# A three-part kernel on TensorE: a new order for the second plan, GpSimd's later start in it, and the last output tile in two halves

## The chip, the cores and the metric

The kernel runs on one core of one Trainium2 chip. The metric is the device time of one execution in microseconds, taken as the median of repeated runs. One further execution is recorded by the hardware profiler; all rows below come from that one. In the rows PE is TensorE's matmuls, PEld its weight loads, DVE is VectorE, ACT ScalarE, POOL GpSimd and SP SyncE.

## The reference

Three layers follow each other; the output of each is the input of the next (float32).

```python
# attention: 4 batches, 8 heads, 576 tokens, 64 wide; block-causal mask in blocks of 64
scores = scale * np.matmul(q, k.transpose(0, 1, 3, 2))
scores = np.where(block_i >= block_j, scores, -1e9)
attn = softmax(scores); x = attn @ v            # reshaped to 2304 tokens x 512
# mixture of experts: 8 experts, 512 -> 1024 -> 512, the two best per token
noisy_logits = x @ w_gate + np.log1p(np.exp(x @ w_noise)) * noise
out[mask] += top2_w[mask, k, None] * (np.maximum(x[mask] @ w1[e], 0.0) @ w2[e])
# dense layer: 512 -> 2048 -> 512
h = x @ w_in
out = (h * np.clip(h + 3.0, 0.0, 6.0) / 6.0) @ w_out
```

## The kernel before

Every large product is made of three matmuls of two rounded parts each: a weight or activation is split into a high part (a cast, `hi`) and a low part (the difference, `lo`), and high x high, high x low and low x high are added up in PSUM. In the names `wah` and `wal` are the two parts of a piece of a first weight matrix, `wbh` and `wbl` of a second one, `xh` and `xl` of a transposed input, `hh` and `hl` of a hidden tile. ScalarE casts the high part of a weight (L408), VectorE or GpSimd subtracts for the low one (L412); L428 and L433 do the same for the input, L480 and L484 for the hidden tile. TensorE's s1 step is L457 to L459 (12 matmuls into a tile `h`), its s2 step L1122 to L1124 (6 matmuls for two token tiles, into tiles `y`).

The program has three stretches. In the first, attention of 16 pairs of heads goes through a first plan: a list scheduler (class `Plan`) that holds for each operation the engines it may run on with a cost, the operations it depends on, and a priority from the table `PR`. It walks through a modelled time, gives each free engine the ready operation of the lowest priority number, and writes the instructions in that order; each engine then runs its own instructions in order, and semaphores keep the dependences. `plan.run` returns the modelled time at which each engine is free.

The second plan begins where the first ends and takes these times as its start (`busy`). It holds three things. The first is the routing of the last batch of tokens (`route`): from the logits `lg` (L870) over softplus, top 2 and one-hot rows to `ohb`, the position matmuls on TensorE (L571 to L575), the selection rows `sel` and `rid`, the matmuls that list each expert's tokens (L616), and from them `ids` (L630). The second is the first 256 columns of expert 0, whose tokens are known from the first three batches: 8 s1 steps, 8 s2 steps, and the splits of its weights. The third follows from the routing: GpSimd gathers the rows of tiles 2 to 4 of expert 0 (L1091), TensorE transposes them (L425, two PSUM tiles in turn); a count of tokens per expert (L1409) leads to `ranks` on VectorE (L1381 to L1392) and `slot_rows` (L1398 to L1403), which fix the order of the experts and the row lists of the others. `PR` gives the priorities of all of these; `wl` picks an entry of `WLS`, the engines on which a weight's low part may run.

```python
WLS = ({"DVE": 1.2}, {"DVE": 1.14, "POOL": 2.4}, {"POOL": 2.4, "DVE": 1.14}, {"POOL": 2.4})
```

After the second plan the order is written out by hand: the rest of expert 0 in 368 columns, experts 1 to 7, then the dense layer. The weights of expert 1 are asked for from ScalarE's queue (L373, L375), its rows by GpSimd's gathers, both with numbers that `ranks` and `slot_rows` made. At the very end `m_s2` scales the four last output tiles from PSUM by 1/6, in turn on VectorE (L1499) and ScalarE (L1497), and SyncE's queue sends each of 256 KB to DRAM (L1502).

Of the kernel before, what the change touches and what calls it, by code (L numbers as in the profile page):

```python
# [7 lines left out]
F32 = mybir.dt.float32  # L8
# [6 lines left out]
OP = mybir.AluOpType  # L15
# [15 lines left out]
YB = 5  # L31
# [12 lines left out]
QSE = ({"DVE": 0.45}, {"POOL": 1.77}, {"ACT": 0.55}, {"DVE": 0.45, "ACT": 0.55})  # L44
WLS = ({"DVE": 1.2}, {"DVE": 1.14, "POOL": 2.4}, {"POOL": 2.4, "DVE": 1.14}, {"POOL": 2.4})
VHS = ({"POOL": 2.3}, {"DVE": 0.42}, {"POOL": 2.3, "DVE": 0.42}, {"DVE": 0.42, "POOL": 2.3}, {"ACT": 0.65, "DVE": 0.42})
PR = {'last': -400, 'ranks': 30, 'rows': -20.0, 'hold': 0.5, 'na': 185.6, 'nb': 352.4, 'lsel': (0, 0, 0, 0, 0, 0, 0, 1, 0, 0), 'f1': (-81.8, 24.7, 6.3, 59.0, -0.2, -63.6, -25.8, 17.6), 'f2': (-4.4, -9.0, -4.1, -76.6, 2.1, -7.1, 6.5, -47.2), 'fa': (-4.3, -4.4, -2.8, 81.4), 'fb': (10.5, -52.7, -45.1, -19.0), 'fh': (-82.6, 22.1, -3.3, -0.4, 24.6, -39.7, -3.6, -72.4), 'fl': (-15.2, 94.0, 43.5, -100.3, 0.8, -76.5, -19.7, 1.6), 'v': -315.73, 'qk': -55.37, 'keep': 1, 'S': 9.04, 'max': -280.34, 'exp': -161.48, 'pt': -15.17, 'hi': 83.56, 'hid': True, 'av': 18.28, 'o': -48.5, 'od': True, 'inv': -240.77, 'fin': 204.7, 'x': -99.74, 'route': 17.68, 'rp': 1, 'route2': -140.2, 'xt': -550.8, 'eg': 594.74, 'ex': 458.19, 'ew': 2239.12, 'first': 0, 'sel': 2, 'vh': 3, 'wl': 1, 'wa': -657.9, 'wb': -101.5, 'h': -105.8, 's2': -43.7, 'vs': (-20.6, 9.99, -35.58), 'vpt': (-0.86, 4.61, -5.4, -4.07, 10.04, 9.83, 18.45, -3.3), 'vp': (57.91, -8.69), 'vf': (23.48, -31.17), 'qe': 1, 'vmax': (-14.96, -14.1, 4.28, -1.49, -1.85, 1.55, -8.85, 4.24, 17.81), 'vexp': (8.68, -1.7, 10.68, 1.91, -0.09, 4.69, -24.46, 2.21, 0.2)}
CLAMP = 122879.9921875


# [7 lines left out]
class Plan:  # L58
# [11 lines left out]
    def add(self, eng, fn, deps=(), prio=0.0, take=None, drop=None, lat=None, after=0.0, port=False, kind=None):  # L70

        if drop is not None:
            drop.left += 1
        self.ops.append((eng, fn, {d for d in deps if d is not None}, prio, take, drop, lat, port, kind))
        self.ready.append(after)
        return len(self.ops) - 1
# [110 lines left out]
def kernel(  # L187
# [14 lines left out]
    nc = tc.nc  # L202
    B, H, S, D = v.shape
    N, DM = out.shape
# [13 lines left out]
    QC = [(0, BLK)] + [(BLK + 128 * i, 128) for i in range((S - BLK) // 128)]  # L218
# [178 lines left out]
    GR = [[(c, 0) for c in (1, 2)], [(c, 0) for c in range(3, NC)] + [(0, b) for b in range(0, B, 2)]]  # L397
# [6 lines left out]
    def split_hi(which, u, new=None):  # L404
        nm = "ab"[which]
        shape = [128, KD, 256] if which == 0 else [128, 2, DM]
        w_s[which, u] = (new or work_tile)(shape, f"w{nm}h"), (new or work_tile)(shape, f"w{nm}l")
        nc.scalar.copy(w_s[which, u][0], raws[PS[u]][which])  # L408
# [44 lines left out]
    yps = {}  # L453
# [43 lines left out]
    def route(b, dep, add, bank, psum, prio0, after=0.0):  # L497
# [8 lines left out]
        def tl(nm, shape=None, dt=F32, bufs=1):  # L506
            T[nm] = g_p.tile(shape or V, dt, tag=nm, name=nm, bufs=bufs)
            return T[nm]

        def step(nm, eng, fn, *deps, **kw):  # L510
            prio[0] += 0.25
            port = nm not in ("ez", "lu", "e2", "top", "ti", "pos", "t", "pi", "idm", "id", "os", "cnt", "short")
            dp[nm] = add(eng, fn, [dp[d] for d in deps] if deps else dep, prio[0], after=after, port=port, **kw)
# [5 lines left out]
        def eng_of(e):  # L519
            return nc.gpsimd if e == "POOL" else nc.vector  # L520
# [82 lines left out]
        for i in range(2):  # L603
# [4 lines left out]
            for c in range(NC):  # L608
                step(f"sel{i}{c}", (SELS[PR["lsel"][i * NC + c]] if last else {"POOL": 0.61}), lambda e, i=i, c=c: eng_of(e).tensor_scalar(
                    tl(f"sel{i}{c}", [128, 128], BF16), laneb, T["pmf"][:, i, c:c + 1], None, op0=OP.is_equal), "pmf")  # L610
# [47 lines left out]
    with actx:  # L658
# [69 lines left out]
        pt, oT, ri, xt = {}, {}, {}, {}  # L728

        def q_scale(e, p, c=(0, S)):  # L730
            o, i = qs[p % 2][:, c[0]:c[1]], raw["q", p % 2][:, c[0]:c[1]]
            if e == "ACT":
                nc.scalar.mul(o, i, qscale)
            else:
                engine(e).tensor_scalar(o, i, qscale, None, op0=OP.mult)

        def scores(p, u):
            q_, k_ = qs[p % 2], raw["k", p % 2]
            for i in ORDER[u]:
                for t, o, a, b_ in SEG[i]:  # L740
                    for h in range(2):
                        r = slice(64 * h, 64 * h + 64)
                        g = h ^ flip(i)
                        nc.tensor.matmul(sb[t][64 * g:64 * g + 64, o:o + b_ - a], lhsT=q_[r, i * BLK:(i + 1) * BLK],
                                         rhs=k_[r, a:b_], start=True, stop=True)
# [3 lines left out]
        def rowmax(p, i, m):  # L749
            if m == 0:  # L750
                nms[p, i] = sm_p.tile([128, len(SEG[i])], F32, tag=f"nm{len(SEG[i])}", name="nm")
            t, o, a, b_ = SEG[i][m]
            nc.vector.tensor_reduce(nms[p, i][:, m:m + 1], sb[t][:, o:o + b_ - a], axis=AX.X, op=OP.max, negate=True)  # L753
# [134 lines left out]
        for p in range(NPAIR):  # L888
            b, j = pairs[p]
            last = p == NPAIR - 1  # L890
# [16 lines left out]
            for m, c in enumerate(FIRST if p == 0 else ((0, S),)):  # L907
                n = c[1] - c[0]
                k["qs", p] = add({"DVE": 0.07 + n / 1500.0} if p == 0 else QSE[PR.get("qe", 0)], lambda e, p=p, c=c: q_scale(e, p, c),
                                 [k.get(("L", "q", p))] + sold, -50 + m if p == 0 else u0 + PR["qk"], after=LAND[m] if p == 0 else 0.0, port=p > 0)  # L910
                ready.append([k["qs", p], k.get(("L", "k", p))])
# [5 lines left out]
            for u in range(NU):  # L917
                U = u0 + u + PR["vs"][u]
                g = Bank(SPOOL[u], 1)
                k["S", p, u] = add({"PE": SCOST[u]}, lambda e, p=p, u=u: scores(p, u),  # L920
                                   ready[0] + (ready[-1] if u else []) + ([k["E", p, i] for i in (0, 1, 3)] if u == 2 else [k.get(("E", p - 1, 7))] if u == 0 else []), U + PR["S"], take=g, kind="S",
                                   after=LAND[min(u, 1)] + 0.1 if p == 0 else 0.0)
                ms, js = {}, {}
                for i in UN[u]:
                    for m, (t, o, a_, b_) in enumerate(SEG[i]):
                        ms[i, m] = add({"DVE": 0.07 + (b_ - a_) / 960.0}, lambda e, p=p, i=i, m=m: rowmax(p, i, m), [k["S", p, u]],
                                       U + PR["max"] + PR["vmax"][i])
                    js[i] = ms[i, 0]
# [31 lines left out]
            hold = add({"PE": 0.0}, lambda e: None, [k["O", p, 0], k["O", p, 1], set_, seti], U, take=gs[0], kind="S")  # L960
# [32 lines left out]
        busy = plan.run({"POOL": 3.6, "DVE": 2.6, "PE": 1.7 + 0.43 * WARM0, "ACT": 2.7, "SP": 2.3})  # L993
# [10 lines left out]
    work = ctx.enter_context(tc.tile_pool(name="work", bufs=2, reuse_waits="tile"))  # L1004
# [340 lines left out]
    def wops(which, u, deps, prio):  # L1345
        if (which, u) in PRE:
            return None
        hi = add({"ACT": 0.95}, lambda e: split_hi(which, u), deps, prio)
        return add(WLS[PR["wl"]], lambda e: split_lo(which, u, e), [hi], prio, port=True)
# [65 lines left out]
        xops(t, k2["g", t], PR["xt"] + t)  # L1415
    wops(0, NPF, [k2["s1", NF - 4], k2["s1", NF - 3]], PR["na"])
    wops(1, NPF, [k2["s2", NF - 4], k2["s2", NF - 3]], PR["nb"])
    plan2.run(busy, PR['last'] + 20, PR['hold'])
    gctx.close()
    wraw2[0] = ctx.enter_context(tc.tile_pool(name="wraw2", bufs=4, side="right", reuse_waits="tile"))  # L1420
# [69 lines left out]
    def m_s2(i, gi, f):  # L1490
        nt = len(GR[gi])
        s2(range(nt), hT.pop(("m", gi, f)), w_s[1, U0 + i], f, f == 0, f == NFF - 1)
        if f == NFF - 1:
            for t in range(nt):
                o = work.tile([128, DM], F32, tag="yo", name="yo", bufs=YB)
                if t % 2:
                    nc.scalar.mul(o, yps[t], 1.0 / 6.0)  # L1497
                else:
                    nc.vector.tensor_scalar(o, yps[t], 1.0 / 6.0, None, op0=OP.mult)  # L1499
                c, b = GR[gi][t]  # L1500
                if c:
                    nc.sync.dma_start(out[b * S + QC[c][0]:b * S + QC[c][0] + 128, :], o)  # L1502
                else:
                    for r in range(2):
                        nc.sync.dma_start(out[(b + r) * S:(b + r) * S + 64, :], o[r * 64:(r + 1) * 64])

    pairs2 = [(gi, p) for gi in range(len(GR)) for p in range(NFF // 2)]
    for i in range(len(pairs2) + 1):
        for r in range(2):
            if i < len(pairs2):  # L1510
                gi, p = pairs2[i]
                f = 2 * p + r
                nt = len(GR[gi + 1]) if gi + 1 < len(GR) else 0
# [11 lines left out]
            if i < len(pairs2) and gi + 1 >= TURNED:  # L1525
                t = (f - 6) // 2
                if f % 2 == 1 and 0 <= t < nt:
                    turned_tile((gi + 1, t, "m"), t, nt * 128, ("m", gi + 1))
                t = (f - 5) // 2
                if f % 2 == 0 and 0 <= t < nt:  # L1530
                    turn_out((gi + 1, t, "m"))
                t = (f - 3) // 2
# [38 lines left out]
```

## Time and profile before

| | |
|---|---|
| three runs | 1014.65 to 1015.74 us, median 1014.91 |
| the profiled execution | 1013.64 us, of which its span (first to last instruction) 1011.8 |
| TensorE busy in the span | 997.2 us (99%), 6813 matmuls |
| VectorE, ScalarE, GpSimd busy | 712.0, 558.3 and 253.4 us |
| mean granted TensorE clock | 0.996 |

A busy TensorE says that a matmul is under way, not that it runs at its peak. Idle time of the other engines costs nothing as such. What counts is where TensorE itself is idle or runs at the lower clock, and which engine's work ended that wait.

### The profile page before, as it was taken

The page shows a single profiled execution, that of the slowest core. Times are in us where ns is not written, and L with a number is a line of the kernel's source. Part 1 is how long each engine was busy: PE and PEld are TensorE (multiplying, and loading weights), DVE is VectorE, ACT ScalarE, POOL GpSimd, SP SyncE. Part 2 cuts the span into 40 slices and gives each one's busy share as a digit, 9 for nine tenths or more (in the row PEclk, how much of TensorE's full clock was granted, in tenths as well). Part 3 has the DMA queues.
Part 4 walks back from the last instruction along what each step waited for, and adds up shares of the span by engine and source line. Part 5 has one row for each costly group of instructions (what it writes and reads, how often), then busy time and mean ns, then how long its engine had stood idle before and what let it go on. Part 6 is the DMA issues. An engine that isn't in the chain of part 4 may idle for free. (4 is left out here: it accounts for less than half of the span.)

```text
span 1011.8 us, 18246 instructions
## 1 busy us (share of the span) xinstructions
PE 997.2 (99%) x6813; PEld 831.7 (82%) x6813; DVE 712.0 (70%) x1396; ACT 558.3 (55%) x1063; POOL 253.4 (25%) x353
## 2 busy tenths in 40 slices
PE   8999998999999999999999999999999999999998
PEld 5667666889889999998888989888888888888886
DVE  6686886767898999887878667757546745754542
ACT  6878785344656565655555356655445445444442
POOL 3255645141020302020200026615204401500000
PEclk9999999999999999999999999999999999999999
DMA  6656542189999999788884263122112202201001
GB/s 155 162 162 158 153 107 56 28 290 326 290 320 285 316 250 303 209 267 196 239 227 150 69 216 104 25 70 48 46 42 63 63 1 74 49 3 42 1 1 42
DMA packets 162745, 141.85 MB, mean 140 GB/s; under 512 B 91541, under 2 KB 130549, under 8 KB 162653
## 3 DMA queue, kind: packets, MB, share of 16 engines
q1 hardware_dynamic: 146669, 102.73, 36.6%
q0 software_dynamic: 8640, 28.32, 9.2%
q10 hardware_dynamic: 7344, 9.60, 2.8%
q8 instruction: 54, 0.88, 0.4%
q14 instruction: 38, 0.31, 0.1%
HBM read 92.91 MB, written 36.70 MB: 128 GB/s over the span
## 5 line engine op out<-in xcount | busy, mean ns | idle before, releaser
L458 PE MATMUL h<-xl,wah 128*128 128x512 f32 (+8 forms) x832 | 272.4, 327 | 3.0 <-DVE xl L433 3.0
L457 PE MATMUL h<-xh,wah 128*128 128x512 f32 (+8 forms) x832 | 273.3, 328 | 1.0 <-DVE lg L870 1.0
L459 PE MATMUL h<-xh,wal 128*128 128x512 f32 (+8 forms) x832 | 272.4, 327 | 0.0
L1122 PE MATMUL y<-wbh,hh 128*128 128x512 f32 (+1 forms) x576 | 226.0, 392 | 0.1
L1123 PE MATMUL y<-wbl,hh 128*128 128x512 f32 (+1 forms) x576 | 225.8, 392 | 0.0
L1124 PE MATMUL y<-wbh,hl 128*128 128x512 f32 (+1 forms) x576 | 225.1, 391 | 0.0
L458 PEld LDWEIGHTS h<-xl,wah 128*128 128x128 f32 x832 | 157.3, 189 | 17.9 <-DVE xl L433 3.4
L457 PEld LDWEIGHTS h<-xh,wah 128*128 128x128 f32 x832 | 157.3, 189 | 16.3 <-ACT wah L408 1.1
L459 PEld LDWEIGHTS h<-xh,wal 128*128 128x128 f32 x832 | 157.4, 189 | 11.5
L480 ACT ACTIVATE hh<-h 128x288 fp32r<-128x288 f32 (+7 forms) x128 | 53.0, 416 | 138.9 <-PE h L459 133.1
L1124 PEld LDWEIGHTS y<-wbh,hl 128*128 128x128 f32 (+1 forms) x576 | 107.5, 187 | 24.6
L1122 PEld LDWEIGHTS y<-wbh,hh 128*128 128x128 f32 (+1 forms) x576 | 107.6, 187 | 21.5 <-issue 0.6
L1123 PEld LDWEIGHTS y<-wbl,hh 128*128 128x128 f32 (+1 forms) x576 | 107.6, 187 | 20.7
L1485 DVE SCALAR_TENSOR_TENSOR r<-r,h 128x512 f32<-128x512 f32 (+1 forms) x80 | 50.4, 630 | 98.5 <-ACT r L1484 98.3
L1484 ACT ACTIVATE r<-h,three 128x512 f32<-128x512 f32 (+1 forms) x80 | 51.6, 645 | 119.0 <-PE h L459 119.0
L412 DVE TENSOR_TENSOR wal<-wa,wah 128x1024 fp32r<-128x1024 f32 x79 | 105.1, 1330 | 12.5 <-ACT wah L408 11.4
L412 DVE TENSOR_TENSOR wbl<-wb,wbh 128x1024 fp32r<-128x1024 f32 x75 | 101.3, 1351 | 14.9 <-ACT wbh L408 11.5
L408 ACT CAST wbh<-wb 128x1024 fp32r<-128x1024 f32 x80 | 83.8, 1047 | 24.8 <-PE y L1124 12.2
L1487 ACT CAST hh<-r 128x512 fp32r<-128x512 f32 (+1 forms) x80 | 46.2, 577 | 84.9 <-DVE r L1485 81.4
L1488 DVE TENSOR_TENSOR hl<-r,hh 128x512 fp32r<-128x512 f32 (+1 forms) x80 | 56.1, 701 | 51.5 <-ACT hh L1487 51.0
L762 ACT ACTIVATE P<-sb,nm 128x288 f32<-128x288 f32 (+8 forms) x160 | 78.7, 524 | 18.7 <-DVE nm L753 18.7
L408 ACT CAST wah<-wa 128x1024 fp32r<-128x1024 f32 x80 | 83.7, 1046 | 2.7 <-DMA wb<-in_moe_w_dram 1.8
(245 smaller groups left out, 1285.2 us busy)
## 6 DMA issues: line engine op xcount, KB each, us to landing
wa<-in_moe_w_dram SPq DMA_DIRECT2D x23, 512.0 KB
wb<-in_moe_w_dram SPq DMA_DIRECT2D x23, 512.0 KB
y_tab<-yo SPq DMA_DIRECT2D x32, 256.0 KB
w<-in_moe_w_in_dram SPq DMA_DIRECT2D x16, 512.0 KB
y_tab<-zero SPq DMA_DIRECT2D x8, 1024.0 KB
w<-in_moe_w_out_dram SPq DMA_DIRECT2D x16, 512.0 KB
wa<-in_moe_w_dram ACTq DMA_DIRECT2D x9, 512.0 KB
wb<-in_moe_w_dram ACTq DMA_DIRECT2D x9, 512.0 KB
```

What stands on the lines that cost most here:

```text
L408: nc.scalar.copy(w_s[which, u][0], raws[PS[u]][which])
L412: (nc.gpsimd if e == "POOL" else nc.vector).tensor_tensor(lo, raws[PS[u]][which], hi.bitcast(F32), op=OP.subtract)
L457: nc.tensor.matmul(ps, lhsT=wh, rhs=xh, start=first, stop=False)
L458: nc.tensor.matmul(ps, lhsT=wh, rhs=xl, start=False, stop=False)
L459: nc.tensor.matmul(ps, lhsT=wl, rhs=xh, start=False, stop=last)
L480: nc.scalar.activation(h[0][:, c0:c1], ps[:, :c1 - c0], AF.Relu)
L762: nc.scalar.activation(P[i][p % PB2][:, a:b_], sb[t][:, o:o + b_ - a], AF.Exp, bias=nms[p, i], scale=1.0, accum_out=rs[p % 3][:, COL[i] + ...
L1122: nc.tensor.matmul(yps[t][:n], lhsT=hh[:, sl], rhs=wh[:, f % 2], start=first, stop=False)
L1123: nc.tensor.matmul(yps[t][:n], lhsT=hh[:, sl], rhs=wl[:, f % 2], start=False, stop=False)
L1124: nc.tensor.matmul(yps[t][:n], lhsT=hl[:, sl], rhs=wh[:, f % 2], start=False, stop=last)
L1484: nc.scalar.activation(r[:, :n], ps[:, :n], AF.Relu, bias=three, scale=1.0)
L1488: nc.vector.tensor_tensor(hl[:, :n], r[:, :n], hh[:, :n].bitcast(F32), op=OP.subtract)
```

## The change

It has three parts. A line ahead of `plan2.run` sets GpSimd's start in the second plan to no sooner than the modelled end of VectorE's work in the first. The numbers of `PR` that belong to the second plan are replaced; among them `wl` goes from 1 to 0, which leaves the low parts of weights to VectorE alone, and `lsel` gives another one of the ten `sel` rows to GpSimd. In `m_s2` the last output tile is scaled in two halves of 256 columns, one by ScalarE and one by VectorE, and sent by two queues.

```diff
-PR = {'last': -400, 'ranks': 30, 'rows': -20.0, 'hold': 0.5,
...
-      'xt': -550.8, 'wl': 1, 'wa': -657.9, 'wb': -101.5, 'h': -105.8, 's2': -43.7,
+PR = {'last': -90, 'ranks': 30, 'rows': -100.0, 'hold': 0.7,
...
+      'xt': -1013.6, 'wl': 0, 'wa': -1003.9, 'wb': 69.6, 'h': -1.0, 's2': -203.8,
...
     wops(1, NPF, [k2["s2", NF - 4], k2["s2", NF - 3]], PR["nb"])
+    busy["POOL"] = max(busy["POOL"], busy["DVE"])
     plan2.run(busy, PR['last'] + 20, PR['hold'])
...
                 o = work.tile([128, DM], F32, tag="yo", name="yo", bufs=YB)
+                c, b = GR[gi][t]
+                if gi == len(GR) - 1 and t == nt - 1:
+                    r0 = b * S + QC[c][0]
+                    nc.scalar.mul(o[:, 0:DM // 2], yps[t][:, 0:DM // 2], 1.0 / 6.0)
+                    nc.scalar.dma_start(out[r0:r0 + 128, 0:DM // 2], o[:, 0:DM // 2])
+                    o2 = work.tile([128, DM], F32, tag="yo", name="yo", bufs=YB)[:, 0:DM // 2]
+                    nc.vector.tensor_scalar(o2, yps[t][:, DM // 2:], 1.0 / 6.0, None, op0=OP.mult)
+                    nc.sync.dma_start(out[r0:r0 + 128, DM // 2:], o2)
+                    continue
                 if t % 2:
                     nc.scalar.mul(o, yps[t], 1.0 / 6.0)
                 else:
                     nc.vector.tensor_scalar(o, yps[t], 1.0 / 6.0, None, op0=OP.mult)
-                c, b = GR[gi][t]
```

What the planner makes of the new numbers shows in the order of the instructions. The first place is VectorE where the second plan begins, as a piece of the difference (- before, + after): `xl_3019` belongs to expert 0's first columns, `zc` and `zx` are the first steps of the last batch's routing.

```order
 L859 TENSOR_TENSOR x<-tb_163,rn_205 128x5x64
 L433 TENSOR_TENSOR xl_3019<-tb_161,xh_3018 128x4x128
-L484 SCALAR_TENSOR_TENSOR hl<-h,hh 128x256
+L412 TENSOR_TENSOR wal<-wa,wah 128x1024
 L528 TENSOR_SCALAR zc<-lg_146 128x40
 L530 TENSOR_SCALAR zx<-lg_146 128x40
-L412 TENSOR_TENSOR wbl<-wb,wbh 128x1024
+L484 SCALAR_TENSOR_TENSOR hl<-h,hh 128x256
 L412 TENSOR_TENSOR wal<-wa,wah 128x1024
```

The routing's first steps now stand ahead of the first `hl`, which waits for TensorE; a weight's low part stands ahead of them. On GpSimd the two L412 rows of the second plan are gone, and nothing else of its order changes but which `sel` it makes. In this stretch TensorE gets four s1 and two s2 steps ahead of the fifth s1 and the position matmuls (L571), where it had two s1, one s2 and three s1.

The second place is TensorE at the end of the second plan; `xps` are the transposes of expert 0's gathered tiles, the first L457 with 128x368 begins its next columns. Before:

```order
L1124 MATMUL y_3142<-wbh,hl 128x512
L425 MATMUL xps<-ident,xn 128x128 x8
L1122 MATMUL y_3138<-wbh,hh 128x512
L1123 MATMUL y_3138<-wbl,hh 128x512
L1124 MATMUL y_3138<-wbh,hl 128x512
L1122 MATMUL y_3142<-wbh,hh 128x512
L1123 MATMUL y_3142<-wbl,hh 128x512
L1124 MATMUL y_3142<-wbh,hl 128x512
L457 MATMUL h<-xh,wah 128x368
```

And after the change:

```order
L1122 MATMUL y_3198<-wbh,hh 128x512
L1123 MATMUL y_3198<-wbl,hh 128x512
L1124 MATMUL y_3198<-wbh,hl 128x512
L425 MATMUL xps<-ident,xn 128x128 x8
L1409 LDWEIGHTS ones
L1409 MATMUL rps<-ohsum_131,ones 128x8
L457 MATMUL h<-xh,wah 128x368
```

The last s2 step has moved from behind the last transposes to ahead of them, and the count for the ranks (L1409) from ahead of the eighth s1 step to behind the transposes.

The third place is VectorE there, as a piece of the difference: the end of the rank block, the low parts of the gathered tiles (`xl`), and the first hidden tile of the 368 columns.

```order
 L1390 TENSOR_TENSOR me<-member,eio 128x64
 L1392 TENSOR_REDUCE order<-me 128x8
-L484 SCALAR_TENSOR_TENSOR hl<-h,hh 128x256
 L1398 SCALAR_TENSOR_TENSOR idf<-idacc 128x40
 L1400 TENSOR_TENSOR idt<-member,idf 128x320
 L1403 TENSOR_REDUCE sids<-idt 128x40
-L412 TENSOR_TENSOR wal<-wa,wah 128x1024
-L433 TENSOR_TENSOR xl<-xps,xh 128x4x128 x3
-L1135 COPY yo<-y_3138 128x512
 L412 TENSOR_TENSOR wal<-wa,wah 128x1024
 L484 SCALAR_TENSOR_TENSOR hl<-h,hh 128x368
```

Before, the three `xl` stood behind the rank block and one low part; now they stand ahead of it, and the block, with one low part, stands between the last `xl` and the first `hl` of the next stage.

## Rows read from the trace of the kernel before

**Rows 1.** Busy time by stage: stretch, PE, PEld, DVE, ACT, POOL, PEclk, DMA share, GB/s

```profile
170.00:210.00 40.00, 33.33 (x231) 29.76 (x221) 29.36 (x97) 15.14 (x26) 13.10 (x10) 0.91 0.19 50
210.00:250.00 40.00, 40.00 (x230) 35.77 (x230) 26.65 (x55) 19.23 (x29) 6.52 (x8) 1.00 1.00 339
250.00:1000.00 750.00, 749.79 (x3902) 645.03 (x3902) 529.51 (x832) 388.59 (x552) 149.72 (x125) 1.00 0.47 135
```

**Rows 2.** TensorE's waits: line, what ended them, us in total, times, longest

```profile
PE h L458 <- DVE xl L433: 3.0, 1, 3.0
PE rps L571 <- DVE ohb L523: 2.5, 1, 2.5
```

**Rows 3.** TensorE alone around its two waits: busy, PEclk, DMA share, GB/s

```profile
174.60:178.00 3.40, 3.13 (x14) 0.50 0.38 87
...
184.80:188.20 3.40, 0.88 (x11) 1.00 0.01 2
188.20:191.60 3.40, 3.40 (x14) 0.51 0.00 0
```

**Rows 4.** Timeline of GpSimd, 171 to 200 us: start, length, instruction, idle before

```profile
171.31 2.41 POOL L412 TENSOR_TENSOR wal<-wa,wah 128x1024 fp32r<-128x1024 f32 x1 [2.90 <-ACT wah L408]
...
196.68 1.63 POOL L1091 DMA_INDIRECT xn<-x_tok,ids  x1 [7.04 <-DVE ids L630]
...
199.88 0.95 POOL L1091 DMA_INDIRECT xn<-x_tok,ids  x1 [0.30 <-issue]
```

**Rows 5.** Timeline of VectorE, 171 to 187 us

```profile
171.27 2.55 DVE L870 TENSOR_TENSOR lg<-lg,x 128x80 f32<-128x80 f32 x2
...
174.14 0.68 DVE L433 TENSOR_TENSOR xl<-tb,xh 128x512 fp32r<-128x512 f32 x1
178.10 0.42 DVE L484 SCALAR_TENSOR_TENSOR hl<-h,hh 128x256 fp32r<-128x256 f32 x1 [3.29 <-ACT hh L480]
178.44 0.18 DVE L528 TENSOR_SCALAR zc<-lg 128x40 f32<-128x40 f32 x1
...
187.09 0.20 DVE L523 TENSOR_TENSOR ohb<-ohs 128x40 bf16<-128x40 f32 x1
```

**Rows 6.** Instructions of the tile lg on VectorE: shortest, median, longest in ns

```profile
L870 DVE TENSOR_TENSOR lg<-lg,x x2: 232/1256/2280, 171.3 to 171.5; 128x80 f32<-128x80 f32 x2
```

**Rows 7.** Timeline of VectorE, 195 to 201 us

```profile
195.47 0.24 DVE L627 TENSOR_TENSOR idacc<-idacc,rps 128x80 f32<-128x80 f32 x1 [1.35 <-PE rps L616]
...
197.76 0.16 DVE L1381 COPY counts<-rps 128x8 f32<-128x8 f32 x1
...
201.17 1.22 DVE L412 TENSOR_TENSOR wal<-wa,wah 128x1024 fp32r<-128x1024 f32 x1
```

**Rows 8.** Timeline of TensorE, 180 to 210 us

```profile
180.50 0.28 PE L457 MATMUL h<-xh,wah 128*128 128x256 f32 x1
...
184.59 0.28 PE L459 MATMUL h<-xh,wal 128*128 128x256 f32 x1
...
198.29 0.40 PE L1122 MATMUL y<-wbh,hh 128*128 128x512 f32 x1
...
201.05 0.60 PE L425 MATMUL xps<-ident,xn 128*128 128x128 f32 x4
...
202.88 1.38 PE L425 MATMUL xps<-ident,xn 128*128 128x128 f32 x8
...
205.66 0.44 PE L458 MATMUL h<-xl,wah 128*128 128x368 f32 x1
...
209.58 0.39 PE L1122 MATMUL y<-wbh,hh 128*128 128x512 f32 x1
```

**Rows 9.** Tail: last scaling on ScalarE (timeline), and busy time by stretch

```profile
1007.90 0.60 ACT L1497 ACTIVATE yo<-y 128x512 f32<-128x512 f32 x1 [0.76 <-PE y L1124]
...
1007.50:1010.00 2.50, 0.37 (x2) 0.00 (x0) 0.42 (x1) 0.60 (x1) 0.00 (x0) 1.00 1.00 382
```

**Rows 10.** Timeline of ScalarE's queue: its first weight request for expert 1

```profile
208.87 0.41 ACTq L373 DMA_DIRECT2D wa<-in_moe_w_dram  x1
```

## What the change will do to the time

> **What bounds the kernel now.** I read the busy time by stage first [rows 1]. From 210 us to 1000 us TensorE is busy in 40.00 of 40 and 749.79 of 750 us at full clock, so nothing that the change moves can shorten that part; it can only start earlier or later. Between 170 and 210 us TensorE is busy for 33.33 of 40 us, at a mean granted clock of 0.91. This is the second plan: the end of attention, the last part of the routing, and the first columns of expert 0. The change rewrites just this stage, and the last output tile. So the question is how many of its 6.7 idle us and of its slow-clock time go, and what new waits come.
>
> TensorE's own waits [rows 2] name two of them: 3.0 us at L458 for VectorE's xl, and 2.5 us at L571 (the position matmuls of the last batch's routing) for VectorE's ohb. The windows of the clock [rows 3] show what follows each: from 174.6 to 178.0 us and from 188.2 to 191.6 us the granted clock is 0.50 (1.2 GHz instead of 2.4). In 188.2 to 191.6 twelve matmuls start, eight of 256 columns and four of 512; at the cadence of the full clock (below) they would take 8 x 0.117 + 4 x 0.23 = 1.9 us instead of 3.4. I price one such stretch at **1.5 us**, bounds 1.3 and 1.7.
>
> Why VectorE is late at 174 us stands in its timeline and GpSimd's. GpSimd starts the low part of a weight (L412, 2.41 us) at 171.31 [rows 4]. VectorE's pair of L870 additions, issued from 171.27, lasts 2.55 us together [rows 5], and by form one takes 232 ns and the other 2280 ns [rows 6]. Same shape, same operands: the second one runs until GpSimd's instruction is over. Behind it stand the x copy and xl, which starts at 174.14 and releases TensorE.
>
> **The change, part by part.** *The line on GpSimd's start time* changes the planner's view alone and adds no semaphore wait. With the new table's wl = 0 the planner may put L412 on VectorE only, and the program built without that line has the same order on every engine. I cost the line at nothing by itself; the table does the work.
>
> *Restart of TensorE.* Without GpSimd's L412 the second L870 takes 0.23 instead of 2.28 us: **-2.05 us**. xl then starts near 172.1 and TensorE's L458 near 172.8. About 0.9 us of that 3.0 us wait stays, and so does the 1 us before L457, which nothing here touches. On GpSimd nothing else stood behind L412 until the sel at 189; the second L412 there (202 us) also leaves. VectorE takes both over, at about 1.13 us each from start to start (the one at 201.17 lasts 1.22 [rows 7]).
>
> *The wait at L571.* Before, VectorE sat idle until hl at 178.10 (3.29 us) and only then began the routing with zc at 178.44 [rows 5]. Now one L412 stands after xl and then zc, so zc comes at 172.1 + 0.6 + 1.13 = 173.8, which is 4.6 us sooner. From zc to the end of ohb took 178.44 to 187.29 = 8.85 us, with three L412 in between; now there are two. ohb is ready between 181.5 and 182.7. TensorE meanwhile runs 59 more matmuls of 256 columns and 12 of 512, six more of the latter than before. Their cadence: 36 matmuls from 180.50 to the last start at 184.59 give 0.117 us; 12 from 198.29 to 201.05 give 0.23 us [rows 8]. 172.8 + 6.9 + 2.8 = 182.5 at full clock, 184.0 with one slow stretch. So the wait goes: **-2.48 us** (bounds -2.3 and -2.48). The cover is thin at full clock; without the six extra matmuls 1.4 us would stay.
>
> *The clock.* A wait of 2.48 us was followed by the slow clock; so were the waits of 1.0 and 3.0 us around L457. After the change the second cause is gone: **-1.5 us**. The first shrinks to about 1.0 + 0.9 us with one matmul in between. No row shows an idle time of that size. Its bounds are 0 (no slow stretch) and 1.5 us. 1.9 us lies nearer to the 2.48 us that did slow the clock than to the idle times under 1 us earlier in the run, where it stayed at full, so I keep one stretch.
>
> *The end of the plan.* Here the new order loses time. After the routing's id matmuls (L616) GpSimd gathers the rows of tiles 2 to 4, and TensorE transposes them. Before, from idacc at 195.47 to the last tile's transposes (the x8 row, 202.88, lasts 1.38 where four last 0.60, so its second four wait 0.43 us and start near 203.66) is 8.2 us [rows 7, 8]; gathers begin at 196.68 and the third at 199.88 [rows 4]. Now TensorE has, between L616 and these transposes, 12 matmuls of 256 columns, 24 of 512 and 8 transposes: 1.4 + 5.5 + 0.7 = 7.6 us. Wait: 0 to 0.7, taken 0.5, since the earlier wait there was not for the gather. Then, before, six y matmuls hid the way from the transposes over xh and xl to the first matmul that reads xl (203.66 to 205.66). Now these six stand ahead of the transposes, and only L1409 and one L457 are left as cover: 2.0 - 0.35 - 0.2 = 1.4 us of wait. Third, VectorE's rank block (197.76 to 201.17 less one hl of 0.34 = 3.1 us [rows 7]) now stands behind the last xl, with an L412 of 1.13 and then the first hl of the next stage behind it: 4.7 us, while TensorE has 23 x 0.17 us from 205.66 to 209.58 [rows 8] and two y matmuls, 4.4 us. Wait 0.3, taken 0.4 (0 to 0.8). Sum +2.3, less the 0.43 us that stood there: **+1.9 us** (1.0 to 2.6).
>
> *The last output tile.* ScalarE's scaling starts at 1007.90 and lasts 0.60; the DMA engines are busy at 1.00, 382 GB/s, from 1007.5 to 1010.0 [rows 9]. The order shows that VectorE's half waits for ScalarE's. A half takes 0.30 to 0.42 on either (hl of 256 columns lasts 0.42 [rows 5]), so the second half ends at 1008.6 to 1008.7 instead of 1008.50. The last transfer is half as long: 128 KB at 382 GB/s is 0.34 us less. The bytes before it are the same and the engines are full. I take **0**, bounds -0.2 and +0.2. The Trainium skill (PSUM — Partial Sum Buffer, PSUM bank collisions raise a hardware error) says that ScalarE and VectorE may not read one bank in the same partitions at once, which would make the halves serial as the order has them. The Trainium skill (Trainium Kernel Development and Optimization, Key Constraints) says that queues of several engines feed the same 16 DMA engines and save issue time alone; by that the second queue gives at most a few tenths, and the sum would be -4.3 instead of -4.1.
>
> *Sum*: -2.05 - 2.48 - 1.5 + 1.9 + 0 = **-4.1 us**. It is made against the profiled execution, 1013.64 us (span 1011.8), which lies 1.27 us below the median of the runs, 1014.91. I apply the difference to the median: **1010.8 us**.
>
> **The rivals.** (A) *No slow clock at the restart.* Speaks for it: the idle time before L458 falls to a third. Against: it still adds up to 1.9 us of 2.3. Another 1.5 us go: 1009.3. (B) *Two slow stretches.* The new waits at the end of the plan (0.5, 1.4 and 0.4 us within some 7 us) bring the clock down again. 1.5 us more, of which the wait for hl absorbs a part: 1011.8 to 1012.3, taken 1012.1. (C) *VectorE is late for L571.* It now carries two more L412, and one of them stands between the maxima and their indices. If ohb came 2.5 us later than I have it, at 185, the wait stayed; 1013.3. Against: VectorE's long idle time before hl is what the new order fills. (D) *Slower.* Expert 1's weights and rows can be asked for only after the rank block, which now starts behind the last xl: at 199 to 200.3 us instead of 197.76. The DMA engines are full from 210 to 250 us (share 1.00, 339 GB/s [rows 1]). If the landing of expert 1's first data set TensorE's start there, the end would come up to 2.5 us later than before, with a slow stretch of 1.5 behind the wait: 1014.9 + 2.5 + 0.5 to 1.5, taken 1017.9. It decides from the point where TensorE asks for expert 1 before its data is there. Against: ScalarE's queue sends the first request at 208.87 [rows 10] behind an hh that waits for TensorE, so the request moves up with TensorE, and TensorE does not idle once in this stretch.
>
> **How the numbers follow.** One slow stretch 0.45; A 0.27; B 0.18; C 0.06; D 0.04. The likeliest gives 1010.8. The range reaches from A with its terms at the good end (1009.3 - 0.7) to B with its terms at the bad end (1012.1 + 0.9): 1008.6 to 1013.0; it leaves out C and D and some of the edges, less than 2 in 10. A measurement of this kernel tells about 0.2%, 2.0 us, from no change. The first three cases lie beyond that but for B's edge: faster 0.86, same 0.10 (C and B's edge), slower 0.04.
>
> **What would show it right or wrong.** In the profile after: no L412 on GpSimd, both L870 near 0.23 us, L458 waiting under 1.2 us; zc near 174 us; no wait, or under 0.5 us, at L571; new TensorE waits at L425 for a gather, at L457 or L458 for xh or xl, and at L1124 for hl; one window at clock 0.50, just after 173 us; the first y matmul of 368-column steps near 205.5 instead of 209.58, and everything after it shifted by the same amount. At the end VectorE's half starts when ScalarE's is over. The forecast is wrong if L870 keeps its 2.28 us, if L571 still waits for 2 us, or if TensorE idles between 210 and 250 us.

## The result

| | before | after |
|---|---|---|
| median of 5 runs | 1015.74 us (1014.65 to 1016.46) | 1006.21 us (1003.85 to 1009.34) |
| the profiled execution, its span | 1013.64, 1011.8 | 1006.84, 1005.0 |

The ratio is 0.9909, with a 95% interval of 0.9888 to 0.9931: some 9.2 us faster by that ratio, where 4.1 was forecast. The time lies under the range of the forecast. I cut both profiled spans at the same four instructions (starts from the timelines of TensorE):

| stretch | before | after | difference |
|---|---|---|---|
| to the first s1 matmul of expert 0 | 171.50 | 171.69 | +0.19 |
| from there to the first y matmul of the 368 columns (the second plan) | 38.08 | 35.92 | -2.16 |
| from there to the first 512-column s1 (the experts) | 441.69 | 442.40 | +0.71 |
| from there to the last matmul (the dense layer) | 356.21 | 350.65 | **-5.56** |
| from there to the end (the tail) | 4.35 | 4.38 | +0.03 |

More than half of the gain lies in the dense layer, where the diff moves nothing, some 440 us behind the plan. I first show that stretch, TensorE alone from 660 to 960 us (stretch, busy and matmuls started, clock, DMA share, GB/s). Before:

```profile
660.00:960.00 300.00, 300.00 (x1305) 1.00 0.15 41
```

After:

```profile
660.00:960.00 300.00, 300.00 (x1325) 1.00 0.16 41
```

The granted clock is 1.00 and TensorE has no idle time in either, and yet 1325 matmuls of 512 columns start where 1305 did. Which of them got faster is told by the groups by form from 660 to 990 us. Before:

```profile
L459 PE MATMUL h<-xh,wal 128*128 128x512 f32 x240 | 94.8, 395 | 0.0
...
L1123 PE MATMUL y<-wbl,hh 128*128 128x512 f32 x238 | 92.9, 391 | 0.0
```

After:

```profile
L1123 PE MATMUL y<-wbl,hh 128*128 128x512 f32 x244 | 95.0, 389 | 0.0
...
L459 PE MATMUL h<-xh,wal 128*128 128x512 f32 x242 | 94.2, 389 | 0.0
```

The s1 matmuls (L459 here; L457 and L458 read 394 before and 389 after) last 389 ns instead of 395, the same as the y matmuls. A matmul starts before the one ahead of it ends, so I read the pace from the starts. Before, one s1 step in the last microseconds, with the two rows of the other engines around it:

```profile
996.36 0.69 DVE L1488 TENSOR_TENSOR hl<-r,hh 128x512 fp32r<-128x512 f32 x1 [0.69 <-ACT hh L1487]
...
996.74 0.40 PE L457 MATMUL h<-xh,wah 128*128 128x512 f32 x1
...
999.53 0.39 PE L1122 MATMUL y<-wbh,hh 128*128 128x512 f32 x1
...
999.79 0.69 ACT L1484 ACTIVATE r<-h,three 128x512 f32<-128x512 f32 x1 [3.46 <-PE h L459]
```

Twelve matmuls take 999.53 - 996.74 = 2.79 us. VectorE's hl is over at 997.05 and ScalarE starts again at 999.79; the step is slow though no other engine computes beside most of it. After:

```profile
805.05 0.39 PE L457 MATMUL h<-xh,wah 128*128 128x512 f32 x1
...
807.77 0.39 PE L1122 MATMUL y<-wbh,hh 128*128 128x512 f32 x1
```

2.72 us, that is 227 ns each instead of 233. By the starts of all 64 steps of the dense layer the mean is 226.6 ns instead of 232.6, which makes 4.6 us; the three y matmuls behind each step, 231.7 ns before, make another 1.0; the two are the 5.56 us.

The second plan. The busy time by stage, where [rows 1] stood before:

```profile
170.00:210.00 40.00, 36.78 (x248) 32.95 (x241) 30.31 (x100) 17.30 (x29) 7.94 (x8) 0.87 0.25 67
210.00:250.00 40.00, 40.00 (x236) 36.08 (x235) 27.28 (x59) 18.35 (x28) 8.29 (x9) 1.00 0.98 333
250.00:1000.00 750.00, 749.55 (x3918) 649.32 (x3917) 529.99 (x832) 389.07 (x552) 148.69 (x125) 1.00 0.48 135
```

These are the columns of [rows 1]. Between 170 and 210 us TensorE is busy for 36.78 us instead of 33.33, at clock 0.87 instead of 0.91. Its waits (line, what ended them, us in total, times, longest), against [rows 2]:

```profile
PE h L458 <- DVE xl L433: 1.1, 2, 0.8
...
PE h L457 <- ACT xh L428: 0.7, 1, 0.7
PE xps L425 <- DMA xn<-x_tok,ids: 0.5, 1, 0.5
```

Two windows of TensorE's clock, against [rows 3]:

```profile
173.00:178.40 5.40, 5.38 (x25) 0.50 0.25 58
...
202.20:205.60 3.40, 3.40 (x12) 0.53 0.45 147
```

VectorE's lg, against [rows 6]:

```profile
L870 DVE TENSOR_TENSOR lg<-lg,x x2: 231/238/245, 171.5 to 171.7; 128x80 f32<-128x80 f32 x2
```

Its timeline, against [rows 5]:

```profile
174.02 0.19 DVE L528 TENSOR_SCALAR zc<-lg 128x40 f32<-128x40 f32 x1
...
176.25 0.42 DVE L484 SCALAR_TENSOR_TENSOR hl<-h,hh 128x256 fp32r<-128x256 f32 x1 [1.95 <-ACT hh L480]
...
184.55 0.20 DVE L523 TENSOR_TENSOR ohb<-ohs 128x40 bf16<-128x40 f32 x1
```

TensorE's timeline, against [rows 2, 8]:

```profile
173.02 0.58 PE L458 MATMUL h<-xl,wah 128*128 128x256 f32 x1 [0.79 <-DVE xl L433]
...
185.32 0.19 PE L571 MATMUL rps<-ohb,before 128*128 128x40 bf16 x1
...
200.08 0.63 PE L425 MATMUL xps<-ident,xn 128*128 128x128 f32 x4 [0.49 <-DMA xn<-x_tok,ids]
...
201.38 0.44 PE L457 MATMUL h<-xh,wah 128*128 128x368 f32 x1 [0.67 <-ACT xh L428]
202.11 0.43 PE L458 MATMUL h<-xl,wah 128*128 128x368 f32 x1 [0.29 <-DVE xl L433]
...
207.61 0.39 PE L1122 MATMUL y<-wbh,hh 128*128 128x512 f32 x1
```

No L870 lasts longer than 245 ns, the wait at L458 is 0.79 us, zc starts at 174.02, and L571 no longer waits. In place of these waits stand 0.49 us at L425 and 0.67 and 0.29 us ahead of the first 368 columns, and the clock is low (1.2 GHz) in two stretches that reach a little beyond or short of the windows shown: from 171.7 to 178.5 and from 202.4 to 205.8 us.

### The profile page after: what moved, and what is told of

Read it like the earlier page. It is cut to its first block, busy times and chain, and to the rows that moved or that the text cites. A ratio compares the mean times of both kernels' runs of the same rounds, so it can differ in the third digit from the quotient of the medians.

```text
span 1005.0 us, 18249 instructions
## 1 busy us (share of the span) xinstructions
PE 993.5 (99%) x6813; PEld 833.9 (83%) x6813; DVE 712.5 (71%) x1399; ACT 558.3 (56%) x1063; POOL 249.1 (25%) x351
## 5 line engine op out<-in xcount | busy, mean ns | idle before, releaser
L457 PE MATMUL h<-xh,wah 128*128 128x512 f32 (+8 forms) x832 | 273.2, 328 | 1.7 <-DVE lg L870 1.0
L458 PE MATMUL h<-xl,wah 128*128 128x512 f32 (+8 forms) x832 | 272.4, 327 | 1.1 <-DVE xl L433 1.1
L459 PE MATMUL h<-xh,wal 128*128 128x512 f32 (+8 forms) x832 | 272.0, 327 | 0.0
L457 PEld LDWEIGHTS h<-xh,wah 128*128 128x128 f32 x832 | 158.4, 190 | 16.3 <-ACT wah L408 1.1
L458 PEld LDWEIGHTS h<-xl,wah 128*128 128x128 f32 x832 | 158.5, 190 | 14.5 <-DVE xl L433 1.6
L459 PEld LDWEIGHTS h<-xh,wal 128*128 128x128 f32 x832 | 158.3, 190 | 10.0
L412 DVE TENSOR_TENSOR wal<-wa,wah 128x1024 fp32r<-128x1024 f32 x80 | 106.3, 1328 | 12.3 <-ACT wah L408 11.4
L412 DVE TENSOR_TENSOR wbl<-wb,wbh 128x1024 fp32r<-128x1024 f32 x76 | 102.5, 1349 | 16.7 <-ACT wbh L408 16.5
```

Of the source, the lines that this page charges most:

```text
L412: (nc.gpsimd if e == "POOL" else nc.vector).tensor_tensor(lo, raws[PS[u]][which], hi.bitcast(F32), op=OP.subtract)
L457: nc.tensor.matmul(ps, lhsT=wh, rhs=xh, start=first, stop=False)
L458: nc.tensor.matmul(ps, lhsT=wh, rhs=xl, start=False, stop=False)
L459: nc.tensor.matmul(ps, lhsT=wl, rhs=xh, start=False, stop=last)
```

## The experiments

### What makes the dense layer faster: SBUF places, PSUM banks, or neither

The order in which a pool's tags are first used decides where their tiles lie. Since the rank block moved behind the last xl, its tags come behind xh, xl and yo in SBUF, and y4's first use moved ahead of y0's. The compiled programs give these places (first byte in each partition; the moving operand is the one that a matmul streams through TensorE, the weights are loaded ahead of it):

```
tile                          before            after
wah (weights of s1)           55744, 59840      55744, 59840
wbh (moving operand of s2)    72128, 76224      72128, 76224
hh, hl (weights of s2)        88512 on          88512 on
off, rt, le, r                119232 on         170432 on
xh (moving operand of s1)     124736, 134976    119232, 129472
xl (moving operand of s1)     145216, 155456    139712, 149952
PSUM banks of y4, y0, y1      4, 2, 3           2, 3, 4
```

Theory S: the place of xh and xl does it. Rivals: the banks (P), or the chip or the run (N). A tile that is asked for and never used is enough to set a place; four kernels on one chip, where the kernel before takes 1014.47 us (18 runs), swap one thing each. For a_sb and b_sb, in `load_x` behind the first `xn`:

```diff
+        if (e, t) == (0, AHEAD):
+            work.tile([128, 16], F32, tag="off", name="key", bufs=1)
+            work.tile([128, E, E], F32, tag="rt", name="gt", bufs=1)
+            work.tile([128, OVF, E], F32, tag="le", name="le", bufs=1)
+            for _ in range(2):
+                work.tile([128, 512], F32, tag="r", name="r")
```

```diff
+        if (e, t) == (0, AHEAD):
+            for nm in ("xh", "xh", "xl", "xl"):
+                work_tile([128, KD, CAP], nm)
+            for _ in range(YB):
+                work.tile([128, DM], F32, tag="yo", name="yo", bufs=YB)
```

For a_ps and b_ps, ahead of `plan2.run`:

```diff
+    for t in range(AHEAD):
+        ps_y.tile([128, DM], F32, tag=f"y{t}", name=f"y{t}")
```

```diff
+    ps_y.tile([128, 512], F32, tag=f"y{NT - 1}", name="h")
```

> The changed kernel, with one thing undone: the SBUF places. In the changed program the tags off, rt, le and r are first used after xh, xl and yo, so that xh, xl and yo lie 5504 bytes lower in each partition (xh at 119232 and 129472 instead of 124736 and 134976). Here these four tags are asked for, without an instruction, right after the first xn, so the places of before come back; the order on every engine stays that of the change, and so do the PSUM banks. Theory S (the SBUF place of xh and xl sets the pace of the s1 matmuls of the dense layer): the s1 matmuls of 512 columns start 233 ns apart again, as before, instead of 227; the dense layer, 1536 matmuls from its first s1 to the last y, takes 355 to 356 us instead of 350.6, and the time is about 5 us above the changed kernel's. Theory P (the PSUM banks of y0 and y1, which moved from 2 and 3 to 3 and 4): no change, 227 ns. Theory N (neither; the chip or the run): no change.

> The changed kernel with the PSUM banks of before alone: y0 and y1 are asked for ahead of the second plan, so y0, y1 and y4 lie in banks 2, 3 and 4 again instead of 3, 4 and 2. Order and SBUF places stay those of the change. Theory S: no change in the dense layer beyond 0.2 us. Theory P: the s1 matmuls go back to 233 ns and those into y0 to 231.5, 5 us more. Theory N: no change.

> The kernel before with the SBUF places of the change: xh, xl and yo are asked for right after the first xn, so xh and xl lie 5504 bytes lower; order and PSUM banks stay those of before. Theory S: s1 matmuls of the dense layer 227 ns apart instead of 233, its 1536 matmuls in about 350.6 us instead of 356.2, and the kernel 5 us faster than before with nothing else touched. Theory P and theory N: no change, 1014.9.

> The kernel before with the PSUM banks of the change: y4 is asked for ahead of y0 and y1 (banks 2, 3, 4 for y4, y0, y1). Order and SBUF places as before. Theory S: at most the three matmuls of y0 change, 192 of them by 5 ns, 1 us together. Theory P: 5 us faster. Theory N: no change.

Measured, the same stretch of TensorE (660 to 960 us) in each. In a_sb:

```profile
660.00:960.00 300.00, 300.00 (x1305) 1.00 0.15 39
```

In a_ps:

```profile
660.00:960.00 300.00, 300.00 (x1325) 1.00 0.15 41
```

In b_sb:

```profile
660.00:960.00 300.00, 300.00 (x1325) 1.00 0.16 41
```

In b_ps:

```profile
660.00:960.00 300.00, 300.00 (x1305) 1.00 0.16 42
```

So 1305 matmuls wherever xh and xl lie as before, and 1325 wherever they lie as after the change, whatever the banks.

| kernel | median, us (runs) | ratio to before, 95% | dense layer, us |
|---|---|---|---|
| a_sb: the change, SBUF places of before | 1010.93 (9) | 0.997 (0.996 to 0.998) | 356.24 |
| a_ps: the change, banks of before | 1007.38 (4) | 0.9931 (0.9914 to 0.9948) | 350.65 |
| b_sb: before, SBUF places of the change | 1009.19 (4) | 0.9952 (0.9935 to 0.9968) | 350.65 |
| b_ps: before, banks of the change | 1014.44 (10) | 1.0001 (0.9991 to 1.001) | 356.20 |

S holds both ways; P and N fall. The new order by itself is worth some 3.5 us in the medians (a_sb; 3.0 by the ratio), the SBUF places alone some 5.3 us (b_sb; 4.9 by the ratio). a_ps, which has both, is 7.1 us under the kernel before on this chip, less than their sum; its runs had the lower mean clocks (0.995 in three of four, where a_sb had 0.998 in most). The 5.56 us of the dense layer belong to the change all the same: they come from the place of the rank block in the order.

### Which property of the place

Other tiles move as well, but two of them can be set aside: r lies 64 above a multiple of 256 before and after, and yo, which moves by as much as xh, is written 17 times in the whole dense layer, too seldom to slow 64 steps. The two places of xh differ in many ways. Within 256 bytes xh stands at 64 before and at 192 after; within 2048 at 1856 and 448. The next three kernels shift xh and all behind it by an unused tile of 64, 128 or 384 bytes (here 64), in the same spot of the changed kernel:

```diff
+        if (e, t) == (0, AHEAD):
+            work.tile([128, 16], F32, tag="pad", name="pad", bufs=1)
```

> The changed kernel with 64 unused bytes per partition ahead of xh, so that xh, xl and yo lie 64 bytes higher: the first xh at 119296, a multiple of 256, instead of 119232 (192 above one; before: 124736, which is 64 above one). Order as in the change. Theory S256 (the place within 256 bytes decides: 192 runs at 227 ns, 64 at 233): a multiple of 256 was not seen yet; I expect 227 ns, and the changed kernel's time within 1 us. Theory S2048 (the place within 2048 bytes decides, 448 fast, 1856 slow): 512 here, 227 expected as near to 448. If it comes slow, neither rule holds as put.

> The same with 128 bytes: the first xh at 119360, which is 64 above a multiple of 256, as before, but 576 above one of 2048. Theory S256: s1 of 512 columns at 233 ns, dense layer 5.5 us longer. Theory S2048: 227 ns, no change.

> The same with 384 bytes: the first xh at 119616, 64 above a multiple of 256, 320 above one of 512 and 832 above one of 1024, all as before, but 832 above one of 2048 where before it was 1856. Theory S256, and one that goes by 512 or 1024: s1 at 233 ns. Theory S2048: 227 ns. Slow here and fast with 128 bytes would mean 512 or 1024.

The same stretch in a_p64:

```profile
660.00:960.00 300.00, 300.00 (x1303) 1.00 0.15 39
```

In a_p128:

```profile
660.00:960.00 300.00, 300.00 (x1305) 1.00 0.15 41
```

In a_p384:

```profile
660.00:960.00 300.00, 300.00 (x1304) 1.00 0.15 41
```

With 128 and 384 bytes the slow pace is back (dense layer 356.2 us in both, one run each), so S2048 falls: the same place within 256 bytes gives the same pace at different places within 512, 1024 and 2048. With 64 bytes I was wrong: a multiple of 256 is slow as well (356.56 us; a_p64 took 1010.85, 7 runs, ratio 0.9962, 0.995 to 0.9975). So 192 is not one of several good places. It is also the place within 256 bytes of everything else that the two steps read (55744, 72128 and 88512 are 192 above a multiple of 256), the weights of s1 among them. That makes two theories: the moving operand's own place (A), or its place relative to the weights (R). One unused tile of 128 bytes ahead of all of them, behind `counts`, tells them apart:

```diff
+    work.tile([128, 32], F32, tag="pad", name="pad", bufs=1)
```

> The changed kernel with 128 unused bytes ahead of all the tiles that s1 and s2 read: wah, wal, wbh, wbl, hh, hl, xh and xl all stand 64 above a multiple of 256 where they stood 192 above one. Theory R (what counts is the place of the moving operand relative to that of the weights): all as in the changed kernel, 227 ns everywhere. Theory A (what counts is the moving operand's own place within 256 bytes): s1 at 233 ns as with 64 before, and now s2 as well, whose moving operand wbh and wbl moves too: 233 ns, the dense layer 9 to 10 us longer.

The same stretch in a_all128:

```profile
660.00:960.00 300.00, 300.00 (x1325) 1.00 0.15 40
```

All at 227 ns, in s1 and in s2 (dense layer 350.65 us, one run): R holds, A falls. The first xh stands at 119360 in a_p128 and in a_all128, slow in one and fast in the other. In numbers, the distance from the weights of s1 to its moving operand within 256 bytes and the dense layer: 0 gives 350.65 us (six kernels), 128 gives 356.2 (six), 64 gives 356.56 (one). R is no rule for each matmul by itself: the y matmuls, whose two operands stand at a distance of 0 in all these kernels, are slow behind a slow s1 step, the first three before (231.7 ns) and in a_p64 most of the twelve (2.77 us instead of 2.72 together). And the kernels do not part the weights of s1 from the other tiles that lie ahead of xh and kept their place with them. Why the hardware behaves so stays open, as does a distance of 192 at 512 columns, which was not tried.

### GpSimd's low parts alone

> The kernel before with one number of the table changed, wl from 1 to 0: the low parts of weights in the second plan on VectorE alone. The planner then writes a new order (on GpSimd only the two L412 go; on TensorE the position matmuls stand earlier, behind five s1 and one s2 step); xh stays at 124736. Theory: the second L870 lasts 0.23 instead of 2.28 us and TensorE waits under 1.2 us at L458 instead of 3.0, 2 us less; the dense layer keeps its 233 ns; the wait at L571 is the open one: fewer matmuls stand ahead of it, and zc comes some 3 us sooner, so 0 to 3 us. Expected 1011 to 1014. Rival (the lock does not come from GpSimd's L412): L870 keeps 2.28 us and nothing goes.

```diff
-      'wl': 1,
+      'wl': 0,
```

VectorE's instructions of the tile lg (shortest, median, longest in ns):

```profile
L870 DVE TENSOR_TENSOR lg<-lg,x x2: 230/236/243, 172.2 to 172.5; 128x80 f32<-128x80 f32 x2
```

TensorE's longest wait in the whole profile:

```profile
PE h L459 <- DVE wal L412: 1.9, 1, 1.9
```

Both L870 are short and the wait at L458 falls to 0.97 us, so what held up (locked) the second L870 was GpSimd's L412. The wait at L571, the open one, does not come. But TensorE then waits 1.9 us for a low part (wal) from VectorE, and the time is 1014.12 us (10 runs; 1014.83 before on that chip), ratio 0.9996 (0.9986 to 1.0006): nothing, and just above the 1011 to 1014 that I expected. Without the rest of the table the 2 us are spent again.

### The low clock, and matmuls that fill the idle places

> The changed kernel itself, beside the next three on the same chip. Expected 1004 to 1009 with a median near 1006, the spread made by how much of the restart at 171 to 179 us and of the plan's end at 202 us runs at granted clock 0.50: the runs so far had a mean clock of 0.994 to 1.000.

> The changed kernel with matmuls that nobody reads in TensorE's two idle places of the second plan: eight bf16 ones of 512 columns into a free PSUM bank behind the last attention matmul, while TensorE waits for lg and xl (1.0 and 0.8 us), and three ahead of the first 368-column step, while it waits for xh and xl (0.7 and 0.3 us). Theory C (the idle time at these two places is what brings the granted clock down to 0.50): no stretch at 0.50 between 170 and 210 us, TensorE's idle time there under 1 us, mean clock 0.999 or more in nearly all runs, and a median 1 to 3 us under the changed kernel's, with less spread. Rival (the clock falls for another reason, as the low share of work in attention's last microseconds): the stretches stay, and the eleven matmuls cost 0 to 0.5 us.

```diff
+    filled = []
+
+    def fill(ps, n):
+        for _ in range(n):
+            nc.tensor.matmul(ps, lhsT=ones, rhs=ones[:, None, :].to_broadcast([128, 4, 128]), start=True, stop=True)
...
+        if (key, f) == (0, 0):
+            fill(ps, 3)
...
+                if not filled:
+                    filled.append(f)
+                    fill(ps_x.tile([128, 512], F32, tag="x", name="fill"), 8)
```

TensorE from 170 to 210 us in after_again (columns as above):

```profile
170.00:210.00 40.00, 36.43 (x267) 1.00 0.34 109
```

In a_fill:

```profile
170.00:210.00 40.00, 38.98 (x275) 1.00 0.36 107
```

The filling in a_fill's timeline of TensorE (L465 are the matmuls that nobody reads):

```profile
170.53 1.90 PE L465 MATMUL fill<-ones 128*128 128x512 bf16 x8
172.08 0.47 PE L457 MATMUL h<-xh,wah 128*128 128x256 f32 x1
172.92 0.39 PE L458 MATMUL h<-xl,wah 128*128 128x256 f32 x1 [0.36 <-DVE xl L433]
...
197.94 0.81 PE L465 MATMUL h<-ones 128*128 128x512 bf16 x3
198.75 0.44 PE L457 MATMUL h<-xh,wah 128*128 128x368 f32 x1
199.47 0.43 PE L458 MATMUL h<-xl,wah 128*128 128x368 f32 x1 [0.29 <-DVE xl L433]
```

Of the 1.77 us of idle time at the restart (0.98 and 0.79 after the change) 0.36 are left; from 170 to 210 us it is 1.02 us in all, where I expected under 1.

a_fill takes 1003.47 us (1003.02 to 1003.95, 4 runs), ratio 0.9884 (0.9868 to 0.9901); the changed kernel on the same chip 1005.46 (1002.67 to 1006.91, 4 runs), ratio 0.9907 (0.989 to 0.9923). All four runs of a_fill had a mean clock of 0.999 or 1.0; of 36 runs with the changed order (any places) 5 had that, 16 had 0.997 or 0.998, and 15 had 0.996 or less. So theory C holds: with the two idle places filled the clock stays (which of the two matters more was not tried). It is also bought: the profiled run of after_again kept the clock by itself (1.00 up to 210 us) with 3.57 us idle, and its span is 1000.9, under a_fill's 1001.2. What the filling gives is a spread of 0.9 us instead of 4.2, and a median that is 2.0 us lower; the two intervals overlap, so against the changed kernel that gain is likely, not shown.

### The last output tile

> The changed kernel with the last output tile scaled whole by ScalarE and sent by one queue, as before. The way from the start of the last matmul to the end of the span was 4.35 us before and is 4.38 with the halves; expected 4.3 to 4.5 here, and no difference in time that a measurement can tell. Rival (the halves save what the second queue and the shorter transfer promise, and something else took it back): 0.3 us longer or more.

```diff
-                if gi == len(GR) - 1 and t == nt - 1:
...
-                    continue
```

After the change, the last rows:

```profile
1000.66 0.39 PE L1124 MATMUL y<-wbh,hl 128*128 128x512 f32 x1
1001.09 0.38 ACT L1500 ACTIVATE yo<-y 128x256 f32<-128x256 f32 x1 [0.76 <-PE y L1124]
1001.50 0.38 ACTq L1501 DMA_DIRECT2D out_dram<-yo  x1
1001.50 0.42 DVE L1503 TENSOR_SCALAR yo<-y 128x256 f32<-128x256 f32 x1 [0.40 <-ACT yo L1500]
1001.95 0.33 SPq L1504 DMA_DIRECT2D out_dram<-yo  x1
```

And without the halves, last matmul and last scaling:

```profile
1000.78 0.39 PE L1124 MATMUL y<-wbh,hl 128*128 128x512 f32 x1
...
1001.21 0.60 ACT L1499 ACTIVATE yo<-y 128x512 f32<-128x512 f32 x1 [0.76 <-PE y L1124]
```

a_tail takes 1006.47 us (4 runs), ratio 0.9909 (0.9892 to 0.9925; 0.9907 for the changed kernel on the same chip); from its last matmul to the end 4.36 us, as before (4.35) and after (4.38). VectorE's half starts at 1001.50, when ScalarE's is over, and ends at 1001.92, 1.26 us behind the start of the last matmul; the whole scaling ends at 1001.81, 1.03 us behind it. From the end of the last scaling to the end of the span it is then 3.12 us with the halves and 3.33 without, as the shorter last transfer would have it: what the halves lose ahead of the transfer they get back in it. The rival falls.

## Why the prediction was wrong

**The step that failed** is in the first paragraph: TensorE busy at full clock from 210 us to 1000 us, "so nothing that the change moves can shorten that part; it can only start earlier or later". Busy at full clock is not at its peak. The s1 matmuls of the dense layer ran at 233 ns where 227 were to be had, and the order of the second plan fixes the places that decide it. The sum had no term for it, the rivals no case; it measured -5.56 us in the profile and, alone, -5.3 us in the median (b_sb). With the places of before the new order gains 3.5 us (a_sb), where 4.1 was forecast for it; that this comes so near is in part luck, since the terms below miss both ways.

**The terms of the plan**, one by one. The long L870: -2.05 forecast, the wait at L458 fell from 3.02 to 0.79, -2.23. Right, and b_wl0 shows its cause, and that by itself it is worth nothing. The wait at L571: -2.48 forecast, and it is gone. The way there was worse than I had it: ohb is ready at 184.75 instead of 181.5 to 182.7, since hl waits 1.95 us for hh at 176.25, while TensorE is at the low clock. The cover held, since the slow matmuls took longer too: TensorE comes to L571 at 185.32 instead of 184.0. The end of the plan: +2.3 of new waits forecast, 0.49 + 0.67 + 0.29 = 1.45 measured; the gather was sized right (0.5), the way over xh and xl 0.96 instead of 1.4, and the wait for hl (0.4) did not come. The clock: one low stretch forecast instead of two, worth -1.5. From the first s1 to the first y of the 368 columns the profiles take 31.9 us with no low stretch (after_again), 33.2 with one of 3.4 us (a_all128), and 35.9 with one of 6.8 and one of 3.4 us (the change); 38.1 before, with two of 3.4. So the forecast's 38.1 - 4.1 = 34.0 for one stretch was 0.8 too high, rival A's 32.5 and rival B's 35.3 lie 0.6 above and 0.6 below what such profiles show, and all three do occur. A short low stretch costs 1.3 us where I had 1.5, and the profiled run after the change has the case that I gave 0.18, with the first stretch twice as long as I had it: there the clock gave nothing back but took some 1.3 us more than before. Together, -2.23 - 2.48 + 1.02 (the new waits less the 0.43 that stood there) + 1.3 = -2.4, against -2.16 in the table. By the mean clocks of the 36 runs, that case was given too little (15 runs at 0.996 or less) and rival A, at 0.27, too much (5 runs).

**The tail**: 0 forecast, +0.03 measured. The halves run one behind the other, as the order showed. By the rule of the Trainium skill on one bank and two engines (PSUM — Partial Sum Buffer, PSUM bank collisions raise a hardware error) they have to; the trace agrees, with VectorE's start at 1001.50 behind ScalarE's end at 1001.47. The Trainium skill (Trainium Kernel Development and Optimization, Key Constraints) says that issuing from several engines saves issue time alone; in a_tail, without the second queue and without the halves, the tail is no longer (4.36 us against 4.38).

**The rivals**: the wait at L571 did not stay (C), TensorE does not idle from 210 to 250 us (40.00 of 40, D). Neither could have given 1006.

## What to carry to other kernels

A change of order also moves tiles, if a pool places each tag where it is first used: list the places of the operands before and after, and read the pace of equal matmuls (starts in a window, or the mean by form) in stages that the change does not touch. Try the moving operand of a matmul of 512 columns at the same place within 256 bytes as its weights; here that alone was worth 5.3 of 1015 us, without an instruction changed. Do not take it over to fewer columns unmeasured: in the experts the same move gains nothing (below). Idle time of a microsecond or two on TensorE may cost more than itself through the clock (1.8 us at the restart, and up to 2.7 us of slow matmuls behind it), and matmuls that nobody reads held it in four runs of four.

## What the runs showed of the hardware

Matmuls of 512 columns (float32r) at full clock start every 227 ns if the moving operand stands at the weights' place within 256 bytes, and on average every 233 ns at a distance of 128 bytes; at 64 the dense layer loses as much (356.56 us), and there the twelve y matmuls behind an s1 step are slower too (2.77 us instead of 2.72), though their own operands did not move. At fewer columns the sign varies: from before to b_sb, by the starts in the experts, the s1 matmuls of 296 columns go from 133.8 to 138.8 ns, those of 304 from 140.0 to 137.8, those of 288 stay at 132.4, and the stretch of the experts takes 442.6 us instead of 441.7; in these steps the first column moves the start as well, and no run parts the two. And equal orders do not bring equal clocks: with the changed order, by the mean clock of the run, it fell somewhere in 31 of 36 runs and stayed up in 5.
